# Four variances on ScalarE, two late transposes by crossbar DMA and a new order in a fused attention and feed-forward kernel

## The chip, the cores and the metric

The kernel runs on one core of a Trainium2 chip. The metric is device time in microseconds, from single executions. A run's time is about 1.75 us longer than the profile's span of the same execution (209.85 against 208.1 for the profiled run of the kernel before; 1.7 to 1.8 in the other profiles of the two kernels).

Names: PE is TensorE, PEld its weight loads, DVE is VectorE, ACT is ScalarE, POOL is GpSimd, SP the queue that issues most DMAs. A "hole" is time in which PE could have started its next product and did not. I count it from the spacing of starts in the trace, less 0.216 us for a product of 512 columns, 0.109 for 256, 0.056 for 128 and 0.031 for 65. The idle time that a timeline prints in brackets is counted otherwise and is some 0.16 us shorter for the same wait. The trace lacks some product records (29 of 2346 in the first profile); a missing one is filled in from its weight load.

## The reference

```
scores = q @ k.T / sqrt(64), masked by 32-wide blocks      # batch 4, 8 heads, 768 x 768
attn   = softmax(scores) @ v                               # -> x: 3072 x 512
h      = x @ w_in                                          # 3072 x 1024
solu   = h * softmax(h)
ln     = (solu - mean(solu)) / sqrt(var(solu) + 1e-6) * g
out    = ln @ w_out                                        # 3072 x 512, fp32
```

## The kernel before

The kernel carries its own planner: operations with an engine, an assumed duration, dependencies, buffers and a due time are placed one after the other, and the program is emitted in the order found. The due times (lists A, F, Q and a shift by kind) were found by search. Attention and feed-forward are interleaved all along. There are 12 tiles of 256 rows of x; each has two halves of 128 rows, so 24 halves. A half of the feed-forward:

```python
xp = ...                       # transposed x: TensorE for the first and the last tile, else crossbar DMA
h  = 8 matmuls x w_in          # "hmm", L579, into two banks of a score buffer (sbank)
se = ACT exp(h), with its sum
so = DVE h * e, with its sum   # L592
ce = DVE so * 1024 - sum       # L596, centred (times 1024)
bn = DVE bn_stats x2           # L599, 512 columns each
mv = DVE bn_aggr               # L602
rs = POOL (var + eps') ** -0.5 # L604, L606, L610
st = transposed ce             # TensorE for the first and the last tile (L554 and a copy, L558), else crossbar
o  = 8 matmuls x w_out         # "outp", L629, into one of two output banks (mbank)
ot = o * rs                    # L640 on DVE, L643 on ACT for the last three tiles
store
...
for _ in range(fillers): nc.tensor.matmul(sbank, onesf, onesf)   # L695, warm-up products in the idle time of the head
```

The very last half is done as two blocks of 256 columns, so that its last eviction and store are shorter.

The softmax here doesn't subtract the row's maximum and nothing guards it: scores larger than these inputs give would overflow.

## Time and profile before

| | |
|---|---|
| time, 3 runs | 214.12 us (213.74 to 214.29) |
| span of the profiled execution | 208.1 us |
| time of that same execution | 209.85 us |
| busy: PE, ACT, DVE | 199.6, 169.9, 157.9 us |
| TensorE transposes of x and solu | 48, of which 24 in the last tile |

### The profile page before, as it was taken

The page shows a single profiled execution, that of the slowest core. Times are in us where ns is not written, and L with a number is a line of the kernel's source. Part 1 is how long each engine was busy: PE and PEld are TensorE (multiplying, and loading weights), DVE is VectorE, ACT ScalarE, POOL GpSimd, SP SyncE. Part 2 cuts the span into 40 slices and gives each one's busy share as a digit, 9 for nine tenths or more (in the row PEclk, how much of TensorE's full clock was granted, in tenths as well). Part 3 has the DMA queues.
Part 4 walks back from the last instruction along what each step waited for, and adds up shares of the span by engine and source line. Part 5 has one row for each costly group of instructions (what it writes and reads, how often), then busy time and mean ns, then how long its engine had stood idle before and what let it go on. Part 6 is the DMA issues. An engine that isn't in the chain of part 4 may idle for free.

```text
span 208.1 us, 5881 instructions
## 1 busy us (share of the span) xinstructions
PE 199.6 (96%) x2317; PEld 144.5 (69%) x2346; DVE 157.9 (76%) x375; ACT 169.9 (82%) x207; POOL 63.1 (30%) x131
## 2 busy tenths in 40 slices
PE   7899999999999999999999999999999999999893
PEld 6599999776768777667677776766776556555342
DVE  4898789897788776782858666679879788698862
ACT  6799999999999899899899999998995775635220
POOL 5135015335531161154311342144110121304230
PEclk9999999999999999999999999999999999999998
DMA  5999987899996799599997969999525565546162
GB/s 171 346 382 367 259 288 100 221 266 279 302 155 166 193 243 187 123 304 211 253 172 198 266 166 155 226 291 242 117 63 113 149 144 103 140 117 104 50 203 101
DMA packets 69263, 41.28 MB, mean 198 GB/s; under 512 B 52204, under 2 KB 64756, under 8 KB 69236
## 3 DMA queue, kind: packets, MB, share of 16 engines
q1 hardware_dynamic: 68640, 39.86, 77.8%
q0 software_dynamic: 544, 1.05, 2.7%
q8 instruction: 18, 0.29, 0.6%
q14 instruction: 9, 0.07, 0.1%
q10 hardware_dynamic: 52, 0.00, 0.0%
HBM read 23.07 MB, written 6.29 MB: 141 GB/s over the span
## 4 chain that ended last, share of the span: by engine, by line
PE 82%; ACT 9%; DMA 3%; issue 2%; DVE 1%; SPq 1%; ACTq 0%
PE sbank L503 27%; PE mbank L629 19%; PE sbank L579 17%; PE mbank L524 15%; ACT ex L514 6%; DMA kst<-in_k_dram 3%; PE mbank L466 2%; ACT eso L588 2%; PE sbank L695 1%; PE mbank L554 1%; SPq L277 1%; ACT ot L643 1%; DVE ot L640 0%; DVE eso L592 0%; DVE kb L444 0%
## 5 line engine op out<-in xcount | busy, mean ns | idle before, releaser
L514 ACT ACTIVATE ex<-sbank 128x1024 bf16<-128x1024 f32 x144 | 138.5, 1034 | 11.3 <-PE sbank L503 10.1
L503 PE MATMUL sbank<-qT,kT 88*128 88x256 bf16 x576 | 85.0, 272 | 1.1 <-ACT ex L514 0.3
L503 PEld LDWEIGHTS <-kT 88*128 88x128 bf16 x576 | 52.5, 97 | 23.4 <-issue 3.2
L579 PE MATMUL sbank<-w_in_sb,xT 128*128 128x512 bf16 x175 | 48.4, 379 | 0.6
L524 PEld LDWEIGHTS <-ex 128*128 128x128 bf16 x1152 | 45.0, 97 | 5.0 <-DVE x L538 0.2
L629 PE MATMUL mbank<-w_out_sb,eso 128*128 128x512 bf16 (+1 forms) x188 | 46.7, 370 | 1.7 <-ACT ot L643 1.2
L524 PE MATMUL mbank<-va,ex 128*128 128x65 bf16 x1152 | 47.2, 193 | 0.0
L592 DVE SCALAR_TENSOR_TENSOR eso<-sbank,eso 128x1024 bf16<-128x1024 f32 x24 | 29.4, 1224 | 13.1 <-ACT eso L588 13.0
L588 ACT ACTIVATE eso<-sbank 128x1024 bf16<-128x1024 f32 x24 | 24.8, 1033 | 11.4 <-PE sbank L579 11.4
L599 DVE BATCH_NORM_STATS2 bn<-eso 128x6 f32<-128x512 bf16 x48 | 30.7, 682 | 0.1
L629 PEld LDWEIGHTS <-eso 128*128 128x128 bf16 x200 | 18.5, 97 | 15.7 <-issue 2.0
L606 POOL TENSOR_SCALAR mv<-se,mv 128x1 f32<-128x1 f32 x24 | 7.1, 298 | 65.2 <-DVE mv L602 60.4
L579 PEld LDWEIGHTS <-xT 128*128 128x128 bf16 x192 | 17.9, 98 | 10.7
L535 DVE RECIPROCAL r<-mbank 128x4 f32<-128x4 f32 x48 | 8.5, 178 | 18.2 <-PE mbank L524 17.9
L538 DVE TENSOR_TENSOR x<-mbank,r 128x256 bf16<-128x256 f32 x48 | 19.9, 415 | 0.6
L640 DVE TENSOR_SCALAR ot<-mbank,rs 128x512 f32<-128x512 f32 (+1 forms) x19 | 14.0, 735 | 8.0 <-POOL rs L610 3.9
L485 POOL CAST va<-vst 128x768 bf16<-128x768 f32 x16 | 13.9, 867 | 18.4 <-DMA vst<-in_v_dram 17.2
L420 POOL CAST kb<-kst 128x768 bf16<-128x768 f32 x12 | 10.1, 840 | 19.3 <-DMA kst<-in_k_dram 18.0
L610 POOL TENSOR_TENSOR rs<-mv,neg_half 128x1 f32<-128x1 f32 x24 | 13.5, 563 | 2.5 <-ACT ot L643 0.6
L420 POOL CAST qb<-qst 128x768 bf16<-128x768 f32 x12 | 10.0, 832 | 12.4 <-DMA qst<-in_q_dram 12.4
L643 ACT ACTIVATE ot<-mbank,rs 128x512 f32<-128x512 f32 (+1 forms) x6 | 3.9, 652 | 10.9 <-PE mbank L629 9.8
L596 DVE TENSOR_SCALAR eso<-eso,mu 128x1024 bf16<-128x1024 bf16 x24 | 11.9, 494 | 0.1
(72 smaller groups left out, 117.2 us busy)
## 6 DMA issues: line engine op xcount, KB each, us to landing
vst<-in_v_dram SPq DMA_DIRECT2D x16, 384.0 KB, 5.2
out_dram<-ot SPq DMA_DIRECT2D x23, 256.0 KB, 2.4
kst<-in_k_dram SPq DMA_DIRECT2D x15, 384.0 KB, 6.1
qst<-in_q_dram SPq DMA_DIRECT2D x15, 384.0 KB, 5.0
w_in_sb<-in_moe_w_in_dram POOLq DMA_DIRECT2D x2, 512.0 KB, 11.6
kT<-in_moe_w_out_dram SPq DMA_DIRECT2D x1, 768.0 KB
qT<-in_moe_w_out_dram SPq DMA_DIRECT2D x1, 768.0 KB, 14.0
eso<-in_moe_w_out_dram SPq DMA_DIRECT2D x1, 512.0 KB
```

The source lines that it names most:

```text
L420: nc.gpsimd.tensor_copy(out=half(cb[o.slot], 0).rearrange("p (c h d) -> p c h d", c=NCH, h=2), in_=st[ld.slot].rearrange("p h c d -> p c h ...
L485: vc = op("POOL", pool_us(S) + 0.3, lambda o: nc.gpsimd.tensor_copy(out=va[i][:, 2 * pr : 2 * pr + 2, :, 0:D], in_=vst[ld.slot]), [ld, von ...
L503: nc.tensor.matmul(s[:, m, :], kT[i][0:DM, pr, hh, jc * P : (jc + 1) * P], qT[i][0:DM, pr, hh, t * TW : (t + 1) * TW], start=(m % 2 == 0), ...
L514: exs.append(op("ACT", act_us(1024), lambda o, so=so: nc.scalar.activation(out=exb[o.slot], in_=sbank[so.slot], func=ACT.Exp, scale=scale) ...
L524: nc.tensor.matmul(acc[:, qt, hh, :], exb[exs[n].slot][:, m, qt * P : (qt + 1) * P], va[i][:, 2 * pr + hh, jc, :], start=(n + m + qt == 0) ...
L538: nrm = op("DVE", 0.41, lambda o: nc.vector.tensor_tensor(out=xb[x_of[(b, t)].slot][:, :, 2 * pr * D : (2 * pr + 2) * D].rearrange("p a (h ...
L579: nc.tensor.matmul(h[:, f * 512 : (f + 1) * 512], xTb[xp.slot][:, a, c, :], w_in_sb[:, c, f * 512 : (f + 1) * 512], start=(c == 0), stop=( ...
L588: se = op("ACT", act_us(d_ff) + 0.22, lambda o, h0=h0: nc.scalar.activation(out=eb[o.slots["e"]], in_=pair(h0), func=ACT.Exp, accum_out=se ...
L592: so = op("DVE", 1.3, lambda o, h0=h0, se=se: nc.vector.scalar_tensor_tensor(out=sob[o.slot], in0=pair(h0), scalar=1.0, in1=eb[se.slots["e ...
L599: bn = op("DVE", 2 * 0.68, lambda o, so=so: [nc.vector.bn_stats(out=bnb[o.slot][:, f], in_=sob[so.slot][:, f * 512 : (f + 1) * 512]) for f ...
L629: nc.tensor.matmul(bank(o0 or o)[:, 0:w], sotb[st.slot][:, f, :], w_out_sb[:, f, col : col + w], start=(f == 0), stop=(f == KF - 1))
L640: nc.vector.tensor_scalar(out=otb[o.slot][:, 0:w], in0=bank(o0)[:, 0:w], scalar1=rsb[rs.slot], scalar2=None, op0=ALU.mult)
```

## The change

Intent: VectorE is nearly full at the end while ScalarE idles, so the variance of the last four halves becomes one ScalarE instruction: a Square with scale 1024^-0.5 and an accumulated sum, which is the mean square of the centred values. Of the last tile's transposes, x and the first solu half go from TensorE to the crossbar. The due times were searched anew. Core of the diff (abridged; the comments after # are mine):

```diff
+    squares = const.tile([P, d_ff], BF16, name="squares")
...
-        if by_pe:
+        if first:
             xp = pe_transpose(...)
...
+            if last:                      # the last two tiles
+                mv = op("ACT", 1.17, lambda o, so=so: nc.scalar.activation(
+                    out=squares, in_=sob[so.slot], func=ACT.Square, scale=d_ff ** -0.5,
+                    accum_out=mvb[o.slot][:, 1:2]), [ce], ...)
+            else:
                 bn = ...; mv = ...        # as before
...
-            if by_pe:
+            if first or last and t == NT - 1 and a:
                 st = pe_transpose(...)
...
-    A = [...]; F = [...]; Q = [...]; SHIFT = {...}
+    A = [...]; F = [...]; Q = [...]; SHIFT = {...}        # all new
```

## The prediction

> **What bounds the kernel now.** I read the page first: the busy digits in 40 slices, to see which engine stays full and when another takes over.
>
> ```profile
> PE   7899999999999999999999999999999999999893
> ...
> DVE  4898789897788776782858666679879788698862
> ACT  6799999999999899899899999998995775635220
> PEclk9999999999999999999999999999999999999998
> ```
>
> PE is at 9 in every slice from the third to the 37th. ACT is as full until about slice 30 (156 us), then falls to 2 to 7: attention's exponentials run out and the feed-forward remainder is left. DVE stays at 8 to 9 late. The clock is full, so no throttle is in play. The change works on the last part, where ACT is idle and DVE is not. The view of stretches gives that in us per 10 us (columns: length, then PE, PEld, DVE, ACT, POOL busy):
>
> ```profile
> 180.00:190.00 10.00, 9.95 (x73) 5.23 (x73) 7.93 (x16) 4.04 (x7) 2.04 (x6) 1.00 0.68 145
> 190.00:200.00 10.00, 9.17 (x50) 4.35 (x49) 9.31 (x20) 3.61 (x6) 2.88 (x8) 1.00 0.34 93
> ```
>
> DVE is busy 9.31 of 10 us, ACT 3.61. That makes the move of variance look attractive. But PE is busy too, and the chain of work that ended last runs nearly wholly through PE there (start, length, what):
>
> ```profile
> 186.60 5.18 PE sbank L579 x24
> 192.21 0.45 PE mbank L554 x8
> 192.71 1.26 PE mbank L629 x5
> 193.99 0.70 ACT ot L643
> 194.73 5.35 PE mbank L629 x24
> 200.16 0.70 ACT ot L643
> 200.90 2.76 PE mbank L629 x16
> 203.69 1.05 PE mbank L629 x8
> 204.88 0.47 ACT ot L643
> ```
>
> L579 is the first feed-forward product, L629 the second, L554 a transpose on TensorE. Of 17.8 us from 186.60 to 204.4, PE leaves only the two ACT evictions as holes. VectorE isn't in these rows at all: its 93% is load beside the path. At the end come the last eviction and its store, about 3.2 us to 208.1.
>
> PE busy is modelled, so I took PE's work from the spacing of starts within the timeline: 24 matmuls of 512 columns in 5.18 us are 0.216 us each; 8 transposes in 0.45 us, 0.056 each; 24 of 65 columns in 0.75 us, 0.031 each; 4 of 256 in 0.44 us, 0.109 each. With the counts of the program (576 scores 62.8, 1152 probability-times-value 35.7, 192 L579 41.5, 184 full L629 39.7 and 16 half ones 1.7, the rest transposes and fillers) PE has about 193.6 us from the first score at 5.9 us. 204.7 - 5.9 = 198.8, so all PE holes after the first score total about 5.2 us. That is the whole stake: 2.5% of the span, and a part of it lies in the head, which is not touched.
>
> **What the Trainium skill says.** (1) "TensorE: Matmul & The Clock Gate", section "Back-to-back issue gap": an isolated gap of N/2.4 + 2.5 ns, 216 ns at N=512. The trace agrees (0.216). The same section gives about 131 ns sustained for weight-load pairs; this trace doesn't show that. (2) "VectorE: DVE Perf Modes", "The three transpose paths": 390 ns for a 128x128 on TensorE against 1309 ns by DMA crossbar. Here eight tiles take 0.45 us of PE plus a 0.69 us DVE copy, against a median of 3.1 us (solu) or 3.8 us (x) from issue to landing: the crossbar has the longer latency, and takes no PE time. (3) "ScalarE: Activation LUTs", "What ACT_TABLE_LOAD costs": 186 ns + 0.833 ns per element with immediates, 1.04 us at 1024; the exponential takes 1.03 us here. Its section on table sets warns of 2.7 us per change of set; the changed program, as built, still has one table load, so Square costs none.
>
> **The change part by part.** Rows of the groups of instructions that price it (busy, mean ns):
>
> ```profile
> L599 DVE BATCH_NORM_STATS2 bn<-eso 128x6 f32<-128x512 bf16 x48 | 30.7, 682 | 0.1
> ...
> L588 ACT ACTIVATION_READ_ACCUMULATOR eso<-sbank 128x1 f32 x24 | 5.0, 210 | 0.0
> ...
> L602 DVE BATCH_NORM_AGGREGATE mv<-bn 128x2 f32<-128x12 f32 x24 | 4.8, 199 | 0.2
> ...
> L558 DVE COPY eso<-mbank 128x1024 bf16<-128x1024 bf16 x4 | 2.8, 688 | 0.6 <-PE mbank L629 0.3 <-PE mbank L554 0.3
> ```
>
> *Variance.* Off DVE: 4 x (1.28 for a pair of statistics + 0.20 aggregate) = 5.9 us. Onto ACT: 4 x (1.04, estimate from the page above, + 0.21 accumulator read) = 5.0 us. All of it lies beside PE; its direct worth is 0. Indirectly, DVE reaches the centring and transposed copies sooner.
>
> *Transposes.* 8 tiles of the last x and 8 of its first solu half leave PE: 16 x 0.056 = 0.90 us, plus a 0.16 us hole ahead of each group (its weight load starts late, seen at 184.5, 191.8 and 199.7): 0.3 us. Also 2 x 0.69 = 1.4 us of DVE copies, and two holds of an accumulator bank. These PE pieces were on the path. Added: two crossbar transposes of 1.24 us issue on the Sync queue.
>
> *Order.* The due times of the whole schedule are new, so every queue is reordered. In the built program, PE work from the first score is 192.8 us against 193.6 (16 transposes fewer, two fillers more): -0.8.
>
> *The end, walked with the durations above.* Zero is the end of the last probability-times-value block, 182.4 us before. Before: 32 L579 (6.9) + 48 full L629 (10.4) + 16 half (1.7) + 24 transposes (1.3) = 20.4 us of work in 22.3 us: 1.9 us of holes. Of these 0.94 is bank waiting for the ACT eviction at 193.99, 0.38 that at 200.16, 0.5 the transposes' weight loads. After, in the new PE order: 26 L579 (5.6) + 56 full L629 (12.1) + 1.7 + 8 transposes (0.45) = 19.9 us. PE holds back finished second products as cover:
> - Last x: division and normalisation on DVE until about 1.4, crossbar issue 1.5, landing 1.5 + 3.8 = 5.3. PE has other products until 5.6. Covered, by only 0.3 us.
> - Last but one solu half: L579 ends 7.3, exponential to 8.7, product to 10.1, an eviction and centring to 11.4, crossbar to about 15. PE reads it at about 16.9. Covered by 2 us.
> - Last half: first products end 10.8, exponential 12.2, DVE to 14.1; TensorE transposes would start at 16.0 but need the bank that ACT empties behind a Square (14.2 to 15.4), so about 16.1 to 16.2: a hole of 0.3.
> - Small holes: 0.16 weight load of these transposes, 0.15 and 0.1 at bank turns.
>
> About 0.7 us of holes in place of 1.9. Sum: work -0.8, holes -1.2, together -2.0 us if the rest of the schedule has the holes that it had. I give back 0.5 us for landings later than the median and for a Square in the ACT queue ahead of an eviction: -1.5 us. The launch constant (214.1 - 208.1) is unaffected.
>
> **Rivals.**
> A. *The crossbar becomes the wait.* The x landing has 0.3 us of cover, and the Sync queue is in order: in the timeline two solu transposes at 165.1 occupied it for 4.74 us instead of 2.5. One such delay ahead of the last x moves the end by 1 to 2 us: time 213.5 to 215.
> B. *DVE was the real bound of the end* (93% there), so relief is worth more: 5.9 + 1.4 us freed. The chain speaks against it: no DVE row in those pieces. The ceiling is the 5.2 us of all holes plus 0.9: under 209 us would need a third engine never to hold PE up. I don't believe more than 3 us: 211.
> C. *Reordering in the middle costs holes.* From 10 to 180 us PE lost only about 0.2 us per 10 us; a new order planned from rounded costs could equally lose 0.3. That is 2 us either way, the widest uncertainty: 211 to 214.5.
> D. *Squares on ACT delay evictions*, since ACT is in order and accumulator banks are two. Each Square of 1.25 us ahead of an eviction may hold PE for up to 1 us; 0 to 1 us, so 212.6 to 213.6.
>
> **Range and chances.** Centre 214.1 - 1.5 = 212.6. All work off PE is 0.4%; 2% faster needs 4.3 us, more than all holes beyond the head, so I give that 4%. Slower by 2% needs 4.3 us of new holes, a schedule that has gone wrong in the middle: 3%. The range from 211.2 (rival B or a lucky middle) to 214.1 (A) should hold 8 in 10.
>
> **What the changed profile would show.** Right: PE at 9 up to the last 3 slices, DVE in the last 20 us down by some 5 to 7 us, ACT up by 5; Square at 1.0 to 1.1 us plus a 0.2 read; 16 fewer L554-type transposes; the 0.94 us hole gone; span near 206.6. Wrong: "DMA xT" named in the chain or in PE's waits near the last first-products (A); a hole of over 0.5 us ahead of the last transposes behind a Square (D); PE holes in the first 150 us grown by over a us (C), or fallen by as much.

## The result

| | runs | us |
|---|---|---|
| before | 4 | 214.29, 214.12, 213.74, 214.05; median 214.09 |
| changed | 4 | 207.53, 211.35, 207.71, 211.40; median 209.53 |

The reported ratio is 0.9699 (0.9676 to 0.9723). Reported ratios compare the fast runs of two kernels in the same rounds, so they are not the ratio of the medians; they lie within 0.001 of the ratio of the means of those runs. "Fast" is judged against the fastest run of the same kernel. The ratio above compares two runs of the changed kernel near 207.6 with four of the kernel before near 214.

The profile speaks of a smaller gain: 205.7 us of span against 208.1, which is 1.2%. The busy rows of the page, changed kernel:

```profile
PE   7899999999999999999999999999999999999993
...
DVE  4997889996788796864848675679887658788720
ACT  6799999999999999889999999998998928456532
```

PE now stays at 9 to the last slice but one. The stretches from 180 to 200 us (length, then busy time of PE, PEld, DVE, ACT, POOL, with the number of instructions in brackets):

```profile
180.00:190.00 10.00, 9.95 (x68) 4.94 (x67) 8.65 (x18) 6.02 (x11) 3.22 (x9) 1.00 0.70 156
190.00:200.00 10.00, 9.49 (x50) 4.52 (x50) 5.35 (x9) 4.69 (x10) 2.84 (x8) 1.00 0.63 186
```

VectorE falls from 17.2 to 14.0 us in these two rows and ScalarE rises from 7.7 to 10.7. Over the whole span VectorE's busy time falls by 5.3 us (157.9 to 152.6; 7.3 were removed, and its longer rows elsewhere took some back) and ScalarE's rises by 4.0. The groups that price the parts:

```profile
L602 ACT ACTIVATE squares<-eso 128x1024 bf16<-128x1024 bf16 x4 | 4.2, 1054 | 1.1 <-DVE eso L597 1.1
...
L602 ACT ACTIVATION_READ_ACCUMULATOR squares<-eso 128x1 f32 x4 | 0.8, 192 | 0.0
```

A Square takes 1.05 us and its accumulator read 0.19: the estimate was 1.04 and 0.21. The chain that ended last, changed kernel (start, length, what; L580 and L636 are the L579 and L629 of before):

```profile
184.26 3.02 PE mbank L636 x14
187.28 2.16 PE sbank L580 x10
189.44 1.73 PE mbank L636 x8
191.16 1.29 PE sbank L580 x6
192.46 0.22 PE mbank L636
192.67 0.05 issue
192.73 4.93 PE mbank L636 x22
197.65 0.03 DVEq L647
197.69 0.05 issue
197.73 0.76 DVE ot L647
198.50 0.04 issue
198.54 3.76 PE mbank L636 x24
```

Both ACT evictions of before (193.99 and 200.16) are gone from it; one DVE eviction at 197.73 is left. From the end of the last probability-times-value block (180.91 + 0.75 = 181.66) to the end of PE's work (198.54 + 3.76 = 202.30) it took 20.64 us. The prediction's walk gave 19.9 us of work and 0.7 of holes, 20.6. So at the end of the profile the total is what was worked out. The time is not: two questions are left. Where do 207.5 and 211.4 come from, and which of them should be set against 214?

### The profile page after: what moved, and what is told of

It is laid out like the page before. It is cut to its first block, busy times and chain, and to the rows that moved or that the text cites.

```text
span 205.7 us, 5857 instructions
## 1 busy us (share of the span) xinstructions
PE 197.6 (96%) x2304; PEld 143.1 (70%) x2332; DVE 152.6 (74%) x361; ACT 173.9 (85%) x215; POOL 63.7 (31%) x131
## 3 DMA queue, kind: packets, MB, share of 16 engines
q0 software_dynamic: 544, 1.05, 2.7%
## 4 chain that ended last, share of the span: by engine, by line
PE 85%; DVE 5%; ACT 4%; issue 2%; DMA 1%; POOL 1%; DVEq 0%; ACTq 0%; POOLq 0%
PE sbank L504 28%; PE mbank L636 20%; PE sbank L580 18%; PE mbank L525 14%; ACT ex L515 3%; DVE w_out_sb L402 3%; PE mbank L467 2%; DMA samp_i<-in_sampled_blocks_dram 1%; PE sbank L703 1%; DVE ot L647 1%; PE mbank L555 1%; ACT eso L589 1%; PE sbank L467 1%; DVE kb L445 1%; DVE x L539 0%
## 5 line engine op out<-in xcount | busy, mean ns | idle before, releaser
L504 PE MATMUL sbank<-qT,kT 88*128 88x256 bf16 x576 | 85.4, 272 | 0.5
L504 PEld LDWEIGHTS <-kT 88*128 88x128 bf16 x576 | 52.2, 97 | 23.0 <-issue 2.1
L580 PE MATMUL sbank<-w_in_sb,xT 128*128 128x512 bf16 x174 | 48.5, 379 | 0.7
L636 PE MATMUL mbank<-w_out_sb,eso 128*128 128x512 bf16 (+1 forms) x190 | 46.5, 370 | 1.0 <-DVE ot L647 0.5
L636 PEld LDWEIGHTS <-eso 128*128 128x128 bf16 x200 | 18.8, 98 | 15.5 <-issue 0.6
L606 DVE BATCH_NORM_STATS2 bn<-eso 128x6 f32<-128x512 bf16 x40 | 25.6, 682 | 0.2
L580 PEld LDWEIGHTS <-xT 128*128 128x128 bf16 x192 | 17.9, 98 | 10.3
L539 DVE TENSOR_TENSOR x<-mbank,r 128x256 bf16<-128x256 f32 x48 | 19.9, 418 | 0.7
L486 POOL CAST va<-vst 128x768 bf16<-128x768 f32 x16 | 14.1, 881 | 17.2 <-DMA vst<-in_v_dram 17.1
L617 POOL TENSOR_TENSOR rs<-mv,neg_half 128x1 f32<-128x1 f32 x24 | 14.4, 602 | 6.6 <-ACT ot L650 3.5
L597 DVE TENSOR_SCALAR eso<-eso,mu 128x1024 bf16<-128x1024 bf16 x24 | 12.5, 523 | 0.2
L611 POOL TENSOR_TENSOR se<-se 128x1 f32<-128x1 f32 x24 | 4.9, 203 | 19.3 <-ACT eso L589 19.1
```

Of the source, the lines that this page charges most:

```text
L504: nc.tensor.matmul(s[:, m, :], kT[i][0:DM, pr, hh, jc * P : (jc + 1) * P], qT[i][0:DM, pr, hh, t * TW : (t + 1) * TW], start=(m % 2 == 0), ...
L539: nrm = op("DVE", 0.41, lambda o: nc.vector.tensor_tensor(out=xb[x_of[(b, t)].slot][:, :, 2 * pr * D : (2 * pr + 2) * D].rearrange("p a (h ...
L580: nc.tensor.matmul(h[:, f * 512 : (f + 1) * 512], xTb[xp.slot][:, a, c, :], w_in_sb[:, c, f * 512 : (f + 1) * 512], start=(c == 0), stop=( ...
L606: bn = op("DVE", 2 * 0.68, lambda o, so=so: [nc.vector.bn_stats(out=bnb[o.slot][:, f], in_=sob[so.slot][:, f * 512 : (f + 1) * 512]) for f ...
L617: rs = op("POOL", 0.55, lambda o, mv=mv: nc.gpsimd.tensor_tensor(out=rsb[o.slot], in0=mvb[mv.slot][:, 0:1], in1=neg_half, op=ALU.pow), [q2 ...
L636: nc.tensor.matmul(bank(o0 or o)[:, 0:w], sotb[st.slot][:, f, :], w_out_sb[:, f, col : col + w], start=(f == 0), stop=(f == KF - 1))
```

## The experiments

All runs below gave correct results. They came in four batches on different chips (e1 to e4; e5 to e8; e9 to e12; e13 to e16). The mean of the early runs of the kernel before was 209.9, 209.7 and 209.9 us in the first three, so a difference of 0.2 us between runs of different batches means nothing. "Early" and "late" runs are the two groups of one kernel's runs, some 4 us apart; e13 to e16 show why they are called so.

### Two groups of runs: e1, e2

Unchanged copies of both kernels.

> The kernel before, unchanged, run as if it were a change. Theory S (two states): every kernel here has a fast state and a slow one some 4 us longer, drawn per run; the first timing of the kernel before drew 4 slow runs (213.7 to 214.3) and its profile one fast run (209.85 us, span 208.1). Then of some ten runs of this kernel here some should be near 209.9 and the others near 214. Rival R (no states; the profiled run of before was the odd one): all runs at 213.7 to 214.3.

> The changed kernel, unchanged. Theory S: runs in two groups, near 207.6 and near 211.4, each 2.3 to 2.8 us below the same group of the kernel before, so a like-for-like gain of 1.1 to 1.3%. Rival R: the kernel before only at 214, so the gain is 3% for the fast runs of this one.

Measured: the copy of the kernel before gave 209.72, 209.41, 209.82, 210.65, 210.40 and one run of 214.17; the kernel before that ran in the same rounds gave four runs of 209.6 to 210.1 and seven of 213.6 to 214.4. The copy of the changed kernel gave 207.60, 207.34, 207.26, 207.40, one of 211.14 and one between, 209.38. Rival R falls: both kernels have both groups. Over all runs of the unchanged kernel before, 24 (the profiled run of 209.85 among them) lie at 209.4 to 210.7 (mean 209.84) and 24 at 213.6 to 215.0 (mean 214.16). The changed kernel: six at 207.3 to 207.7 (mean 207.47), five at 211.1 to 211.5 (mean 211.37), one between, 209.38, which stays unexplained and is left out of both means here. Like with like the change is worth 2.4 us in the first group (ratio 0.9887) and 2.8 us in the second (0.9870). The 3% of the first measurement set one group against the other.

### What the groups are: e13 to e16, one look each

Single profiled runs of unchanged copies, to catch the slower group in a profile.

> One look at the kernel before. Theory H: if its time is near 214, its profile has the clock granted after 12 us and the extra 4 us lie before 20 us; if near 210, the clock at 5 to 6 us. Rival C (slow from outside): a slow profile with the early clock, its 4 us spread over the span or in the transfers.

> A second draw of the same: near 214 with the clock granted after 12 us, or near 210 with it at 5 to 6 us (theory H); a slow run with an early clock would speak for rival C.

> One look at the changed kernel. Theory H: near 211.3 with the clock after 12 us, or near 207.5 with it at 5 to 6 us, and nothing else different after 20 us. Rival C as for the kernel before.

> A second draw of the same: near 211.3 with the clock granted after 12 us, or near 207.5 with it at 5 to 6 us (theory H); a slow run with an early clock would speak for rival C.

Measured: 209.38 and 214.11 for the kernel before, 211.48 and 211.49 for the changed one. So both kernels were caught in the slower group. Stretches of the head, kernel before, its first profile (208.1 us; columns as above, then PEclk, DMA share, GB/s):

```profile
8.00:12.00 4.00, 3.58 (x48) 2.98 (x48) 3.39 (x10) 3.45 (x4) 0.39 (x2) 1.00 1.04 375
12.00:16.00 4.00, 4.00 (x70) 3.77 (x68) 3.92 (x9) 3.95 (x5) 1.88 (x3) 1.00 1.07 378
20.00:24.00 4.00, 4.00 (x64) 3.50 (x61) 2.39 (x7) 3.66 (x5) 0.00 (x0) 1.00 1.10 262
```

The same kernel in the look that took 214.11 us:

```profile
8.00:12.00 4.00, 4.00 (x31) 2.56 (x29) 2.77 (x8) 2.34 (x3) 0.69 (x1) 1.00 1.02 363
12.00:16.00 4.00, 4.00 (x30) 3.42 (x29) 2.26 (x6) 2.58 (x3) 1.69 (x3) 1.00 1.06 374
20.00:24.00 4.00, 4.00 (x74) 3.81 (x71) 3.19 (x8) 3.91 (x5) 0.00 (x0) 1.00 1.09 266
```

From 12 to 16 us PE is "busy" for 4.00 of 4 us in both, but starts 70 products in the one and 30 in the other. DMA moves about the same (378 and 374 GB/s). From 20 us on the late run is no longer behind (64 and 74). The column PEclk says 1.00 throughout: the trace holds no clock record before the first grant, and the column counts such time as full, so in this stretch it is no evidence. The spacing of starts is. Chain of the changed kernel in the look of 211.48 us:

```profile
14.72 0.64 PE mbank L467 x6
15.36 0.85 PE sbank L504 x4
16.21 0.43 PE sbank L703 x4
16.64 0.64 PE mbank L467 x6
17.28 0.60 PE sbank L504 x4
17.88 0.34 PE mbank L467 x6
18.21 0.44 PE sbank L504 x4
```

Four score products (L504) take 0.85 us up to 16.2 us and 0.44 from 18.2 on, six transposes (L467) 0.64 and then 0.34: half speed until about 17.4 us, full speed after. The same chain in the changed kernel's first profile (205.7 us):

```profile
14.81 0.44 PE sbank L504 x4
15.25 0.34 PE mbank L467 x6
15.58 0.44 PE sbank L504 x4
```

Full speed. In that profile PE's starts are at full speed from about 5 us on. The trace's clock records say the same: full clock granted at 4.7 to 5.8 us in the quick profiles of these two kernels, at 17.3 to 17.5 us in the three slow ones. In all eighteen traces each recorded stretch at full clock lasts a whole number of 3.413 us (201.386 us, or 59 of them, in the quick profiles of these two kernels, 56 or 57 in the slow ones). From 20 us on, holes in quick and slow profiles agree within 0.5 us in nearly every 10 us. Theory H holds: the groups are an early and a late grant of the TensorE clock, drawn per run, and the late one costs 4.3 us of the kernel before and 3.9 of the changed one. The first timing of the kernel before drew four late runs, and its profile an early one.

### The warm-up products taken away: e6 and e9, and a denser head: e5

e6 is the changed kernel, e9 the kernel before, each without its warm-up products ahead of the first scores:

```diff
-                for _ in range(max(0, int((o.start - idle) * SPARE / ...))):
+                n = max(0, int((o.start - idle) * SPARE / ...))
+                for _ in range(0 if o.start < COLD else n):
```

e5 is the changed kernel with four more of them, in the hole at 3.8 us:

```diff
+                for _ in range(n + 4 if 2.5 < o.start < 4.6 and n > 1 else n):
```

> The changed kernel with four more warm-up products (11 in place of 7) in the idle 0.4 us at 3.8 us, ahead of the first key transposes; nothing else differs. Theory H: the slow state is a TensorE clock that is granted late in the head (5 to 6 us in fast profiles, 18.07 us in a slow one), so a denser head makes slow runs rarer: of six runs 0 or 1 slow, median 207.2 to 208. Rival C: the slow state comes from outside (memory, the chip) and does not ask for the head: a third to a half of the runs stay near 211.

> The changed kernel without its 20 warm-up products before the first scores. Theory H: the clock is granted late in every run, so every run is slow or slower, 211 to 213 us, and its profile shows half clock until 10 us or later. Rival C: two groups as before, 207.6 and 211.4, in about the same shares.

> The kernel before, without its warm-up products ahead of the first scores, to be set against the changed kernel without its own (211.2 us, late clock in its profile at 17.16 us). Theory H: the clock comes late in nearly every run of this one too, so all runs lie in one group near the slow runs of the kernel before, 213 to 214.5 us, and the change is worth 2.3 to 3 us with the start of the clock held alike (1.1 to 1.4%). If the change really were worth 3% in every state, this one would be at 217 to 218.

Measured: e6 210.29 to 212.04 (mean 211.33), e9 213.23 to 214.06 (mean 213.66). Neither has an early run, and each sits near its parent's late runs. The profile of e6 shows half speed until about 17 us (four score products, L504):

```profile
15.03 0.85 PE sbank L504 x4
17.89 0.44 PE sbank L504 x4
```

and that of e9 until about 14.3 (L503):

```profile
13.01 0.85 PE sbank L503 x4
14.72 0.44 PE sbank L503 x4
```

Between these two the change is worth 2.33 us: ratio 211.33 / 213.66 = 0.9891. That agrees with the like-for-like figures above, but it is no cleaner than they are: the two ran in different batches, and in their profiles the clock came 2.9 us apart (17.16 and 14.24), so it was kept from coming early and not held alike.

e5 missed: four of six runs were late by their times (212.4 to 212.7) and the two early ones (208.65, 209.54) were above the changed kernel's. In its profile the first scores start at 6.60 us instead of 6.1 to 6.2. So the warm-up products are needed for an early grant, but a denser head did not make it more frequent, and my explanation by density finds no support. Six runs are a small draw: e7 below, with the head of the changed kernel, had six early of six. What decides the draw is open.

### The change taken apart in code and order: e3, e4

e3 has the old code with the new due times, e4 the new code with the old ones. Both are planned anew, so every queue is reordered.

> The code before (statistics on DVE, transposes on TensorE as before) with the new due times alone. If the gain comes from the freed work (theory P: 16 transposes and their holes off PE, DVE relieved), this order doesn't fit the old work and the fast state is at or above the kernel before: 209.5 to 212 us. If it comes from the new order (theory Q), the fast state is 207.5 to 208.5.

> The changed code with the old due times, planned anew by the kernel's own planner. Theory P: the 0.9 us of transposes and part of the holes are gone, fast state 208.3 to 209.3. Theory Q: no gain without the new order, or a loss at the end where crossbar latency is not covered: 209.5 to 211.

Measured, early runs: e3 211.45 to 212.35 (mean 212.0), e4 211.97 to 212.65 (mean 212.3). Each alone is 2.2 to 2.4 us slower than the kernel before, together they are 2.4 us quicker. For e3 the first expectation (209.5 to 212) nearly holds; e4 missed both of its own (208.3 to 209.3, 209.5 to 211). Why the new code fails in the old order is seen in PE's timeline of e4 (the last bracket is idle time before, and what ended it):

```profile
193.50 3.18 PE L636 MATMUL mbank<-w_out_sb,eso 128*128 128x512 bf16 x13
199.81 1.03 PE L555 MATMUL mbank<-ident,eso 128*128 128x128 bf16 x8 [3.12 <-DVE eso L597]
200.64 6.84 PE L636 MATMUL mbank<-w_out_sb,eso 128*128 128x512 bf16 x32
```

PE stands idle for 3.12 us, for want of finished products to fill the time in which the last halves pass through ACT and DVE. After the idle time the eight transposes take 0.83 us to the next start, 0.104 each: half speed again, until 203.2 us by the clock records, 3.41 us after the restart. The hole is paid for twice.

### Each part alone, planned anew: e10, e11

e10 keeps the transposes' change and the new due times, with the statistics on VectorE (`if last:` becomes `if False:`). e11 keeps the Squares and puts the last tile's transposes back on TensorE.

> Last x and last but one solu half by crossbar, statistics kept on VectorE, new due times, planned anew. From e7 (statistics back on VectorE in fixed places cost nothing in the fast state) the transposes and the order carry the gain: fast state 207.3 to 208.3. If VectorE's relief is what lets the planner hide the crossbar: 208.5 to 210.

> Squares on ScalarE, transposes on TensorE as before, new due times, planned anew. Prediction (variance is worth 0 by itself): fast state at that of the kernel before or above it, 209.3 to 211.5, since 16 transposes are back and the due times were found for another program. If the variance carries the gain: 207.5 to 208.5.

Measured, early runs: e10 210.26 to 210.50 (mean 210.39, ratio 1.0022), e11 211.26 to 211.91 (mean 211.59, ratio 1.0081). Neither part alone, under these due times, beats the kernel before. e11 was expected at or above it; e10 missed both of its figures (207.3 to 208.3, which I favoured, and 208.5 to 210). Its profile, a late run, has the last transposes wait for VectorE, 1.5 us by the spacing of starts:

```profile
205.13 0.41 DVE eso L597
205.54 0.05 issue
205.59 0.62 PE mbank L555 x8
206.21 3.60 PE mbank L636 x24
```

The planner, which still had the statistics on VectorE, had put the deferred output products ahead of the last tile's first product and had nothing left for this wait. This test mixes the part with a new plan. The next one does not.

### Each part priced in a fixed order: e7, e8

e7 is the changed kernel in its own order, but the four Squares are emitted as statistics on DVE at the same places:

```diff
-                mv = op("ACT", 1.17, lambda o, so=so: nc.scalar.activation(out=squares, ...Square...), ...)
+                mv = op("ACT", 1.17, lambda o, so=so: [nc.vector.bn_stats(out=bnx[:, f], ...) for f in range(2)]
+                    + [nc.vector.bn_aggr(out=mvb[o.slot], in_=bnx)], ...)   # planned as before, emitted on DVE
```

e8 is the changed kernel with the PE time of the 16 transposes put back as products without a use:

```diff
                     def outp(...):
+                        if last and not a and not n:
+                            for _ in range(8):
+                                nc.tensor.matmul(bank(o)[:, 0:P], onesf, onesf, start=True, stop=True)
```

> The changed kernel in its own order, with the four Squares of ScalarE turned back into statistics on VectorE at the same places of its queue; PE's queue is the same. Prediction's claim (the variance move lies beside PE, direct worth 0): fast state within 0.5 us of the changed kernel. Rival B (in this end VectorE sets the pace once PE's cover is tuned to it): three of the four pairs sit ahead of the centring of a last half or of the eviction that frees a bank, at 1.48 us each, so the fast state is 2 to 4 us longer, 209.5 to 211.5.

> The changed kernel with 16 products of 128 columns added to PE, 8 ahead of each of two of the last output groups, into the bank that the group then overwrites: the PE time of the 16 transposes taken away, without their copies or waits. If PE is the bound of the end (prediction): +0.9 us, fast state 208.3 to 208.7. If the end waits for something else (B, or landings): under +0.3.

Measured: e7 207.40 to 208.69, all early, mean 208.08: 0.6 us above the changed kernel's early mean of 207.47, with overlapping runs. Set against the kernel before in its own batch the changed kernel is 2.5 us quicker (e2) and e7 1.6, a difference of 0.9. So the variance move, with the order of all queues kept, is worth 0 to 0.9 us. The 2 to 4 us of rival B fall: the statistics I took to be in the way mostly ran in time in which VectorE waits in the changed kernel (1.15 and 2.28 us of waits between 192 and 198 us, where e7 has two sets of 1.5 us). What is left shows in the idle time before the last long output group. e7:

```profile
197.59 0.75 DVE L647 TENSOR_SCALAR ot<-mbank,rs 128x512 f32<-128x512 f32 x1
198.26 0.68 DVE L559 COPY eso<-mbank 128x1024 bf16<-128x1024 bf16 x1
198.39 1.89 PE L636 MATMUL mbank<-w_out_sb,eso 128*128 128x512 bf16 x8 [0.82 <-DVE ot L647]
```

and the changed kernel:

```profile
197.73 0.75 DVE L647 TENSOR_SCALAR ot<-mbank,rs 128x512 f32<-128x512 f32 x1 [2.28 <-PE mbank L636]
198.40 0.68 DVE L559 COPY eso<-mbank 128x1024 bf16<-128x1024 bf16 x1
198.54 3.75 PE L636 MATMUL mbank<-w_out_sb,eso 128*128 128x512 bf16 x24 [0.45 <-DVE ot L647]
```

The eviction that frees the bank sits behind the last statistics in e7, so PE waits 0.82 us in place of 0.45 (0.99 and 0.62 by the spacing of starts).

e8: 208.30, 208.35 and 208.46 early (mean 208.37), three late at 212.1 to 212.6. That is 0.9 us above the changed kernel, just the 16 x 0.056 us of added PE time (1.2 if counted like e7, as e8 is 1.3 us quicker than the kernel before in its batch). PE is the bound of the end: work put on it there comes back one to one, within some 0.3 us.

### The last hole taken away: e12

The 0.45 us hole is a wait for one of two output banks, while two score banks are idle by then. In e12 the first half of the last tile accumulates there (abridged; the products and the eviction are pointed at the same bank, and no queue changes its order):

```diff
-                            take=None if n else "m", ...
+                            take=None if n else ("sh" if last and t == NT - 1 and not a else "m"), ...
```

> The changed kernel, whose last hole on PE (0.46 us at 197.9, waiting for an eviction to free one of two output banks) is taken away: the last but one output half accumulates in an idle score bank. If PE is the bound to the end: 0.4 to 0.7 us less in the fast state, 206.8 to 207.1, with no hole over 0.2 us after the last transposes. If something else ends the kernel: no change.

Measured: early runs 206.09, 206.75, 207.22 (mean 206.69, ratio 0.9847 to the kernel before), late 210.2 to 211.1. The chain has no eviction in it before the last one:

```profile
192.87 5.18 PE mbank L639 x24
198.05 0.45 PE mbank L558 x8
198.49 1.73 PE sbank L639 x8
200.22 1.76 PE mbank L639 x16
```

This version beats both kernels, by 0.8 us the changed one and by 3.2 us the one before, early runs against early runs. The hole that went was 0.62 us by the spacing of starts; the three early runs spread over 1.1 us, so the 0.2 us above it are not explained and may be noise.

## Why the prediction was right or wrong

The predicted time, 212.6 us in 211.2 to 214.1, is wrong. The measured median is 209.5, the verdict is faster, and I had given that 4%. Both come from mixed groups: the median lies between two early and two late runs, near none of them, and the 3% sets early runs against late ones. Like with like the gain is 1.1 to 1.3%, short of 2%, as the prediction held.

**The step that failed** is the sentence "The launch constant (214.1 - 208.1) is unaffected." Those 6.0 us are not a constant. They are 1.75 us of launch and 4.3 us by which a late clock grant lengthens a run: 214.1 was the time of late runs, 208.1 the span of an early one (e1, e14). With the true constant my own span of 206.6 would have given 208.4 us for early runs, where 207.5 was measured. The information was there before: the profiled run's own time of 209.85 stood beside its span. I also wrote "The clock is full, so no throttle is in play" from the clock row; that row doesn't show the late grant, the spacing of starts in the head does.

**A term of the sum was mis-sized.** For early runs I had -1.5 us, and 2.4 were measured (2.33 between e6 and e9). I had worked out -2.0 and then gave back 0.5 for landings later than the median and for a Square ahead of an eviction. Neither came: the last x was issued at 182.9 and no hole precedes the products that read it, and in the walked part holes were 20.64 - 19.9 = 0.7, as stated. The rest lies in the middle: from 20 us to the last probability-times-value block PE's holes add to 3.2 to 3.7 us in three early profiles of the kernel before, and to 2.7 and 3.0 in two of the changed one (late profiles: 3.3, and 2.4 to 2.5). A new plan could have cost as much (rival C).

**What was misread on the way.** PE starts its first score at 6.25 us and not 5.9, and its work from there, counted again with the prediction's own prices, is 191.6 us and not 193.6. So the holes before were 6.7 us and not 5.2, and the stake was larger than stated. The difference of work (-0.8) is right. The 0.16 us hole ahead of each group of transposes is not in the trace: at 184.48, 191.84 and 199.69 the first transpose starts 0.216 us after the product before it.

**What held.** PE bounds the end: e8, 0.9 us for 0.9 us. The transposes' worth of 0.9 us: the same run. The total of the end: 20.6 us predicted and 20.64 measured. The variance "lies beside PE; its direct worth is 0": in a fixed order 0 to 0.9 us (e7). The hole of 0.94 us is gone. That the 0.7 us of holes came out is in part luck: neither the hole that I put ahead of the last transposes (0.3 us, behind a Square) nor that of their weight load (0.16) is there, and one after them makes up for both (0.62 us by the spacing of starts, behind a DVE eviction).

**The rivals.** A (the crossbar becomes the wait) did not happen in the new order. B (VectorE as the bound) falls by e7. C went the other way: the middle lost about 0.6 us less (0.9 in late profiles). D did not show. None of the four named two kinds of runs.

The code and its order could not be had apart: e3, e4, e10 and e11 all lie 0.5 to 2.5 us above the kernel before, the whole 2.4 us below. My sum added the parts as if each had its own worth. That it came near is owed, I think, to the walk having been done on the new order and not on the diff.

## What to carry to other kernels

Before a profile's span is used with a timing, check that the profiled run's own time is one of the timed ones; here it was not (209.85 against 213.7 to 214.3), because there were two states, and both kernels had to be compared in the same one. A busy row and a clock row can look full while PE runs at half speed: count the starts per microsecond in the head. Where PE was the bound, 0.9 us of work put back on it cost 0.9 us (e8); taking it off paid only in an order that covered the longer latency in its place (e4 lost 2.4 us without).

## What the Trainium skill lacked or had wrong

- "TensorE: Matmul & The Clock Gate", "Part 1: The HAM clock gate": it calls the penalty of the ramp under 1% of a typical span, and the warm-up a budget of about 3.4 us. Here half speed lasted to about 17.4 us in late runs and cost 4.3 of 214 us (2.0%), in 24 of 48 runs of one kernel. That the window is free-running, as the page says, fits runs of one program that differ; four more warm-up products did not make early grants more frequent (4 of 6 late). How busy a window must be to count as busy is not on the page and not settled here.
- The same page, "Back-to-back issue gap": about 131 ns sustained per 512-column product with its weight load. In these traces 24 of them take 5.18 us, 216 ns each, the page's isolated figure.
- The same page, "Part 4: PE-mode transpose": about 275 ns as the duration of a transpose in one kernel's context. Here one lasts 219 ns on average, and in a row they start 56 ns apart at full clock and 107 ns in the late head. What a row of them costs PE is this spacing, which the part does not give.
- "VectorE: DVE Perf Modes", "The three transpose paths", gives 1309 ns for one 128x128 tile by crossbar. For eight tiles SBUF to SBUF no page has a latency: here 3.1 us median for solu, and for x 3.0 to 6.6 us with medians of 3.8 and 4.7 us in two profiles.
- "ScalarE: Activation LUTs", "What ACT_TABLE_LOAD costs", holds for Square (1.054 us at 1024 columns against 1.04), but no page has the duration of ScalarE's separate accumulator read, 0.19 to 0.21 us.
